# A new searched order for a planned one-core kernel, with VectorE and GpSimd kept apart in the search's model

## The chip, the cores and the metric

One core of a Trainium2 chip. The time is that of the core from the first to the last instruction plus launch, in device microseconds (us), median over a few runs. TensorE is called PE in the profile, VectorE DVE, ScalarE ACT, GpSimd POOL. A run is called slow when it is over 1.5% above the fastest run of the same kernel.

## The reference, cut

```python
# r, k, v, w: (4, 8, 768, 48); u: (8, 48)
for t in range(S):                         # linear attention with decay
    cur = einsum('bhd,bhe->bhde', u * k[t], v[t])
    y[t] = einsum('bhd,bhde->bhe', r[t], state + cur)
    state = w[t][..., None] * state + einsum('bhd,bhe->bhde', k[t], v[t])
x = y as (batch, seq, 384)
theta = x @ w_theta                        # wave mixing
y2 = w_tok_r @ (x * cos(theta)) + w_tok_i @ (x * sin(theta))
u = x + y2
out = u + relu(u @ w_ch)
```

The kernel splits each of the four batches into six chunks of 128 steps, numbered 0 to 23. Per chunk it takes a logarithm of the decay (ACT), cumulative sums of it (PE), exponentials of these (ACT), products with r and k (POOL), transposes and small matmuls (PE, copied and masked by DVE), a bonus term u*k*r, and the chunk's output x. Then theta, sine and cosine, the products z (DVE), token mixing, channel mixing, store.

## The kernel before

The program is not written in its final order. Every step is registered with durations and a priority; a planner simulates the engines while the kernel is built and so fixes the order on each engine, and for some steps which engine runs it.

```python
class Planner:
    def op(self, eng, dur, fn, deps=(), alloc=(), free=(), mode=None, prio=0.0, name="", alts=(), pen=0.0):
        key = self.key(name)                       # kind of step and batch: 'z@0', 'beta@0', ...
        penalty = self.penalty.get(key, ...)       # PENALTY: when to take the other engine
        ...
        prio += self.shift.get(key, ...)           # SHIFT: earlier or later in the order
    def order(self, window):
        ...
            first = min(cand, key=lambda q: q[0])          # the step that can start first in the model
            lim = first[0] + window.get(eng, 0.0)          # WIN: how long an engine may wait for a better one
            t, o, eng, dur, i = min((q for q in cand if q[2] == eng and q[0] <= lim),
                                    key=lambda q: (q[1].prio, q[1].i))
```

Each engine works through its queue in this order, and waits where the next step can't start yet. The other part is one accumulator of two PSUM banks, "cum". Its second bank also holds the eight columns of the bonus sums ("beta"), and the "fillers" write to it: matmuls whose result nobody uses, put into TensorE's gaps to keep its clock up. They are put in after the order is fixed, so the planner does not simulate them.

```python
pads["cum"] = [pps.tile([L, 2, 512], f32, tag="cum", name="cum")]
pads["beta"] = [pads["cum"][0][:, 1, DM:DM + H]]             # DM = 384, H = 8
...
def f_cum():                                                  # PE, L435 to L439
    nc.tensor.matmul(cm[:, 0, :DM], ...); nc.tensor.matmul(cm[:, 1, :DM], ...)
def f_exp():                                                  # ACT, L444: reads both banks
    nc.scalar.activation(get(a), get(cum)[:, :, :DM], AF.Exp)
def f_beta(...):                                              # PE, L775: bonus sums into cum's second bank
    nc.tensor.matmul(get(bt), lhsT=get(rkT)[:, j, :], rhs=ublk[:, j, :], ...)
o_bc = P.op("DVE", 0.08, f_rub, [o_beta], [], [bt], ..., name=f"bc{n}",
            alts=[("ACT", 0.1, f_rub_a, 0.0)])                # bonus copy: L780 on DVE, L783 on ACT
o_bon = P.op("POOL", 0.79, f_bon, [o_bc, o_v[i]], ...)        # bonus product, L788
wps = pads["cum"][0][:, 1, DM:]
def fill():                                                   # filler, L1073
    nc.tensor.matmul(wps, lhsT=warm[:, 0, :], rhs=warm[:, 1, :], start=True, stop=True)
```

## Time and profile before

| | before |
|---|---|
| median of 3 runs | 170.01 us (168.47 to 171.23) |
| span of the profiled run, mean granted clock | 168.1 us, 0.984 |
| VectorE busy in all / before 40 us | 132.3 / 26.9 us |
| logarithm of chunk 7 / exponential of chunk 6 start | 24.8 / 23.0 us |
| first z product starts | 38.1 us |

### The profile page before, as it was taken

How to read it: one execution, taken by the hardware profiler on the slowest of the kernel's cores; microseconds unless marked ns; L12 is line 12 of the kernel's file. 1: busy time of each engine (PE TensorE's matmuls, PEld its weight loads, DVE VectorE, ACT ScalarE, POOL GpSimd, SP SyncE). 2: the span in 40 equal slices, each digit the busy share in tenths (PEclk: the TensorE clock that was granted, in tenths of full speed). 3: DMA queues.
4: the chain of work that ended last, by engine and by line, in shares of the span. 5: the costliest groups of instructions: out<-in, count | busy, mean ns of one | idle time of the engine just before them, and what ended most of it. 6: DMA issues, size and time to landing. Idle time of an engine off the chain costs nothing.

```text
span 168.1 us, 5063 instructions
## 1 busy us (share of the span) xinstructions
PE 153.9 (92%) x1986; PEld 103.7 (62%) x1986; DVE 132.3 (79%) x287; ACT 116.0 (69%) x264; POOL 112.4 (67%) x133
## 2 busy tenths in 40 slices
PE   7997798995898999999999999999899999999981
PEld 7575476763665676657566677666566666666640
DVE  4506958899999988797899998899988997436361
ACT  3556585699889997667998696489979963932000
POOL 7198488997986689866367989999979921000000
PEclk9959999999999999999999999999999999999997
DMA  4999999897989999999999999897911101020312
GB/s 102 277 261 248 252 258 177 161 285 174 272 227 215 268 244 281 258 284 216 207 188 206 251 179 221 168 223 142 236 41 47 49 4 66 30 97 0 140 47 94
DMA packets 93769, 29.81 MB, mean 177 GB/s; under 512 B 88369, under 2 KB 92210, under 8 KB 93746
## 3 DMA queue, kind: packets, MB, share of 16 engines
q1 hardware_dynamic: 93344, 29.50, 79.2%
q8 instruction: 15, 0.25, 0.6%
q14 instruction: 8, 0.07, 0.2%
q10 hardware_dynamic: 402, 0.00, 0.1%
HBM read 24.78 MB, written 4.72 MB: 175 GB/s over the span
## 4 chain that ended last, share of the span: by engine, by line
PE 71%; DVE 11%; ACT 8%; POOL 3%; DMA 2%; issue 2%; ACTq 0%; POOLq 0%
PE bank L978 25%; PE bank L1005 7%; PE bank L941 4%; DVE sb_z L955 4%; PE cum L1073 3%; PE bank L611 3%; PE bank L548 3%; PE bank L992 2%; DMA in_w<-in_w_dram 2%; PE bank L606 2%; PE bank L530 2%; PE bank L532 2%; PE bank L632 2%; PE bank L1054 2%; PE cum L435 2%
## 5 line engine op out<-in xcount | busy, mean ns | idle before, releaser
L978 PE MATMUL bank<-sb_z,wtokT 128*128 128x384 bf16 x288 | 53.8, 326 | 0.0
L978 PEld LDWEIGHTS <-wtokT 128*128 128x128 bf16 x288 | 26.0, 98 | 14.9
L524 POOL TENSOR_TENSOR sb_bon<-sb_v,sb_rub 128x384 bf16<-128x384 bf16 x18 | 14.9, 829 | 13.5 <-DVE sb_rub L520 5.5
L955 DVE TENSOR_TENSOR sb_z<-x_all,sb_sc 128x768 bf16<-128x768 bf16 x24 | 20.2, 858 | 1.6 <-ACT sb_sc L949 1.6
L463 POOL TENSOR_TENSOR sb_q<-in_r,sb_a 128x384 bf16<-128x384 f32 x18 | 18.6, 1035 | 2.8 <-ACT sb_alt L449 2.4
L457 POOL TENSOR_TENSOR sb_k<-in_k,sb_a 128x384 bf16<-128x384 f32 x18 | 18.6, 1032 | 1.4 <-DMA in_k<-in_k_dram 1.4
L508 POOL TENSOR_TENSOR sb_ru<-in_r,u_bc 128x384 f32<-128x384 f32 x18 | 19.2, 1069 | 0.2
L987 DVE TENSOR_TENSOR sb_un<-bank,x_all 128x384 bf16<-128x384 f32 x24 | 13.3, 554 | 7.6 <-PE bank L978 7.3
L444 ACT ACTIVATE sb_a<-cum 128x768 f32<-128x768 f32 x18 | 14.8, 824 | 4.2 <-PE cum L439 2.7
L515 POOL TENSOR_TENSOR sb_ruk<-sb_ru,in_k 128x384 bf16<-128x384 f32 x16 | 17.2, 1075 | 0.5
L327 ACT ACT_TABLE_LOAD x12 | 15.4, 1283 | 1.5 <-PEq L1089 1.3
L1005 PE MATMUL bank<-wch,sb_uT 128*128 128x384 bf16 x72 | 15.5, 327 | 0.6 <-DVE sb_uT L999 0.5
L1010 DVE SCALAR_TENSOR_TENSOR sb_o<-bank,sb_un 128x384 f32<-128x384 f32 x24 | 13.2, 553 | 3.6 <-PE bank L1005 3.3
L1073 PE MATMUL cum<-warm 128*128 128x128 bf16 x106 | 11.6, 262 | 4.4 <-ACT sb_rub L783 1.8
L949 ACT ACTIVATE sb_sc<-bank,hpi 128x384 bf16<-128x384 f32 x24 | 14.7, 612 | 0.0
L941 PE MATMUL bank<-wth,sb_xT 128*128 128x384 bf16 x72 | 14.0, 326 | 0.3 <-ACT sb_sc L949 0.3
L536 DVE COPY sb_qkt<-bank 128x1024 bf16<-128x1024 bf16 x18 | 12.3, 684 | 1.6 <-PE bank L532 1.5
L946 ACT ACTIVATE sb_sc<-bank 128x384 bf16<-128x384 f32 x24 | 12.4, 516 | 1.4 <-PE bank L941 1.3
L996 ACT ACTIVATE sb_uT<-bank 128x384 bf16<-128x384 bf16 x14 | 7.0, 503 | 9.0 <-PE bank L992 8.9
L636 ACT ACTIVATE sb_xT<-bank 128x384 bf16<-128x384 bf16 x15 | 7.3, 496 | 8.3 <-PE bank L632 8.3
L553 DVE TENSOR_TENSOR sb_p<-bank,mask_exc 128x512 bf16<-128x512 f32 x18 | 12.3, 683 | 0.6 <-PE bank L548 0.5
L594 ACT ACTIVATE sb_S<-bank,sb_alt 128x48 bf16<-128x48 f32 x52 | 11.6, 323 | 1.7 <-PE bank L584 1.7
(135 smaller groups left out, 341.4 us busy)
## 6 DMA issues: line engine op xcount, KB each, us to landing
out_dram<-sb_o SPq DMA_DIRECT2D x24, 192.0 KB, 2.6
in_w<-in_w_dram SPq DMA_DIRECT2D x18, 192.0 KB, 4.9
in_r<-in_r_dram SPq DMA_DIRECT2D x18, 192.0 KB, 4.8
in_k<-in_k_dram SPq DMA_DIRECT2D x18, 192.0 KB, 4.5
in_v<-in_v_dram SPq DMA_DIRECT2D x18, 192.0 KB, 4.5
sb_w<-in_moe_w_tok_r_dram SPq DMA_DIRECT2D x6, 384.0 KB, 4.9
sb_w<-in_moe_w_tok_i_dram SPq DMA_DIRECT2D x6, 384.0 KB, 5.2
in_w<-in_w_dram SPq DMA_DIRECT2D x3, 384.0 KB, 5.0
```

The costliest lines, as they stand in the source:

```text
L327: nc.scalar.preload_act_table_set(name)
L444: nc.scalar.activation(get(a), get(cum)[:, :, :DM], AF.Exp)
L457: nc.gpsimd.tensor_tensor(get(kk)[:, :, :D], s["x_k"](), av(1), op=ALU.mult)
L463: nc.gpsimd.tensor_tensor(get(q)[:, :, :D], s["x_r"](), av(0), op=ALU.mult)
L508: nc.gpsimd.tensor_tensor(get(ru), s["x_r"](), u_bc, op=ALU.mult)
L515: nc.gpsimd.tensor_tensor(get(ruk), get(ru), s["x_k"](), op=ALU.mult)
L524: nc.gpsimd.tensor_tensor(get(bon), get(vb), get(rub).to_broadcast([L, H, D]), op=ALU.mult)
L941: nc.tensor.matmul(get(th), lhsT=get(s["xT"])[:, j, :], rhs=wth[:, j, :], start=(j == 0), stop=(j == NJ - 1))
L955: nc.vector.tensor_tensor(get(zb[b])[:, c], xb, get(sc), op=ALU.mult)
L978: nc.tensor.matmul(get(ac), lhsT=wtokT[:, q_, s_, ti, :], rhs=get(zb[b])[:, s_, q_, :], start=(s_ == 0 and q_ == 0), stop=(s_ == NCH - 1 a ...
L1005: nc.tensor.matmul(get(ml), lhsT=get(uT)[:, j, :], rhs=wch[:, j, :], start=(j == 0), stop=(j == NJ - 1))
L1073: nc.tensor.matmul(wps, lhsT=warm[:, 0, :], rhs=warm[:, 1, :], start=True, stop=True)
```

## The change

The intent: an order from a new search, in whose model a two-operand VectorE product and a GpSimd instruction exclude each other. What the program gets of it is other priorities (135 of 197 keys of SHIFT, 28 of 41 of PENALTY), other windows and load slacks, and a filler that stays off the bonus columns.

```diff
-    SHIFT = {... 'beta@0': 6.96, 'k@0': -9.79, 'ln@0': 5.4, 'v@0': 1.16, 'xc@0': 0.36, 'z@0': -4.98 ...}
+    SHIFT = {... 'beta@0': 10.46, 'k@0': -15.3, 'ln@0': 6.56, 'v@0': 6.14, 'xc@0': 3.41, 'z@0': -8.2 ...}
-    PENALTY = {... 'bc@0': -0.71 ...}          # bonus copies of the opening: on ACT
+    PENALTY = {... 'bc@0': 0.63 ...}           # ... on DVE
-    SLACK = (3.98, 6.1)
+    SLACK = (4.97, 6.65)
-    WIN = {'PE': 0.1, 'ACT': 0.11, 'DVE': 0.16, 'POOL': 0.39, 'SP': 0.1}
+    WIN = {'PE': 0.0, 'ACT': 0.27, 'DVE': 0.17, 'POOL': 0.0, 'SP': 0.38}
-    wps = pads["cum"][0][:, 1, DM:]
+    wps = pads["cum"][0][:, 1, DM + 2 * H:]
-        nc.tensor.matmul(wps, lhsT=warm[:, 0, :], rhs=warm[:, 1, :], start=True, stop=True)
+        nc.tensor.matmul(wps, lhsT=warm[:, 0, :], rhs=warm[:, 1, :L - 2 * H], start=True, stop=True)
```

(SHIFT and PENALTY are cut; "@0" is the first batch.)

More of the change, by code (lines that the diff above doesn't have):

```diff
@@ L212 @@
     OFF = {'ln': -2.2, 'cum': -2.1, 'exp': -2.05, 'alt': -2.04, 'q': -1.5, 'k': -1.45, 'v': -1.2, 'ru': -1.3, 'ruk': -1.2, 'rub': -1.2, 'bon': -1.1, 'tqk': -0.9, 'qkt': -0.9, 'p': -0.8, 'm0': -0.7, 'pc': -0.7, 'sel': -1.6, 'y': -0.5, 'x': -0.5, 'xt': -0.4, 'xc': -0.4, 'rk': -1.3, 'rkt': -1.2, 'rkc': -1.2, 'beta': -1.15}
-    SHIFT = {'M': -0.23, 'M@0': 3.78, 'M@1': -8.79, 'M@3': 4.37, 'Mp@0': 5.06, 'S': -3.32, 'S@0': 0.3, 'S@1': 4.4, 'S@3': -1.39, 'Sp@0': -0.82, 'alt': -2.71, 'alt@0': -6.46, 'alt@1': -5.24, 'alt@3': -1.0, 'bc@0': 2.73, 'beta@0': 6.96, 'bon': -7.28, 'bon@0': -11.25, 'bon@1': -1.68, 'bon@3': -15.43, 'cos': -4.6, 'cos@0': -8.64, 'cos@1': -3.05, 'cos@3': -4.08, 'cum': 2.98, 'cum@0': -0.21, 'cum@1': -0.34, 'cum@3': 0.03, 'cumo@0': -2.52, 'cump@0': 0.81, 'cwch': 2.19, 'cwch@1': 0.17, 'cwt': -0.63, 'cwt@1': -5.35, 'cwth': 0.26, 'cwth@1': -10.14, 'exk@0': 3.3, 'exp': -7.56, 'exp@0': -8.69, 'exp@1': -7.51, 'exp@3': -3.91, 'exq@0': -3.62, 'fin': 10.83, 'fin@0': 10.28, 'fin@1': 11.48, 'fin@3': 1.68, 'k': -2.66, 'k@0': -9.79, 'k@1': -1.84, 'k@3': 3.21, 'ldk': -0.07, 'ldk@0': 0.25, 'ldk@1': 0.18, 'ldk@3': -0.13, 'ldkp@0': -0.23, 'ldr': -0.52, 'ldr@0': -1.79, 'ldr@1': -1.7, 'ldr@3': -1.11, 'ldrp@0': -0.32, 'ldv': 0.27, 'ldv@0': 0.93, 'ldv@1': 0.57, 'ldv@3': 1.39, 'ldvp@0': 0.18, 'ldw': -1.63, 'ldw@0': -1.67, 'ldw@1': -2.55, 'ldw@3': -1.18, 'ldwp@0': -6.51, 'ln': -1.02, 'ln@0': 5.4, 'ln@1': -2.53, 'ln@3': 2.0, 'm': 1.57, 'm@0': 15.82, 'm@1': 14.98, 'm@3': 17.21, 'ml': 3.16, 'ml@0': -6.88, 'ml@1': -11.74, 'ml@3': -9.39, 'p': 4.22, 'p@0': 8.66, 'p@1': 17.51, 'p@3': 5.23, 'pc': 1.07, 'pc@0': 1.12, 'pc@1': -0.89, 'pc@3': -3.49, 'pp@0': -0.08, 'q': -0.33, 'q@0': -1.43, 'q@1': -1.77, 'q@3': 2.32, 'qkt': 1.93, 'qkt@0': 3.15, 'qkt@1': -5.42, 'qkt@3': -1.23, 'qktp@0': -4.05, 'rk@0': 4.47, 'rkc@0': 2.84, 'rkt@0': -3.15, 'ru': -2.75, 'ru@1': 3.2, 'ru@3': 4.03, 'rub': 1.54, 'rub@1': 3.87, 'rub@3': 6.62, 'ruk': -0.11, 'ruk@1': 4.75, 'ruk@3': 0.58, 'sel': 1.06, 'sel@0': 2.59, 'sel@1': 1.72, 'sel@3': -2.89, 'sin': 1.45, 'sin@0': 7.58, 'sin@1': 1.41, 'sin@3': 6.75, 'st': 0.43, 'st@0': -2.07, 'st@1': 5.27, 'st@3': -5.11, 'th': -5.14, 'th@0': -13.68, 'th@1': -11.99, 'th@3': -7.44, 'toE': -2.74, 'toE@0': 1.79, 'toE@1': 3.28, 'toE@3': 5.51, 'toS': -2.78, 'toS@0': 4.03, 'toS@1': 1.52, 'toS@3': 0.01, 'tok': -3.84, 'tok@0': -14.49, 'tok@1': -16.93, 'tok@3': -11.95, 'tqk': -0.37, 'tqk@0': -7.47, 'tqk@1': -3.98, 'tqk@3': -6.14, 'ubc': 3.86, 'ubc@1': -1.26, 'ublk@1': 12.81, 'ubm': 3.03, 'ubm@1': -0.13, 'uc': -4.81, 'uc@0': -0.8, 'uc@1': 1.76, 'uc@3': 5.44, 'un': 2.42, 'un@0': 3.41, 'un@1': 1.64, 'un@3': 0.26, 'ut': -3.32, 'ut@0': -11.88, 'ut@1': -17.65, 'ut@3': -16.65, 'v': 1.33, 'v@0': 1.16, 'v@1': 4.38, 'v@3': 2.97, 'wch': -0.56, 'wch@1': 4.47, 'wev': 2.67, 'wev@1': 3.64, 'wt': 0.86, 'wt@1': 1.37, 'wth': 0.4, 'wth@1': 0.12, 'wtr': 0.92, 'wtr@1': 4.43, 'x': 1.16, 'x@0': -4.58, 'x@1': -2.03, 'x@3': 1.47, 'xc': 1.62, 'xc@0': 0.36, 'xc@1': 6.08, 'xc@3': 2.79, 'xp@0': -4.33, 'xt': 0.48, 'xt@0': -1.77, 'xt@1': 4.35, 'xt@3': 2.35, 'y': -0.38, 'y@0': -2.78, 'y@1': 3.73, 'y@3': 5.0, 'yp@0': -0.46, 'z': -1.82, 'z@0': -4.98, 'z@1': -4.18, 'z@3': -2.79}
@@ L214 @@
-    PENALTY = {'S': 1.09, 'S@0': 1.12, 'S@1': -0.94, 'S@3': -3.96, 'bc@0': -0.71, 'bon@0': 2.38, 'cwch': -1.71, 'cwch@1': 2.81, 'cwt': 1.34, 'cwt@1': 3.16, 'cwth': 1.85, 'cwth@1': 0.93, 'k': 9.17, 'k@0': 10.47, 'k@1': 3.58, 'k@3': 6.59, 'pc': -1.22, 'pc@0': -2.79, 'pc@1': -4.91, 'pc@3': -5.2, 'qkt': 3.99, 'qkt@0': -0.11, 'qkt@1': 0.97, 'qkt@3': 1.62, 'qktp@0': 2.76, 'rk@0': 7.24, 'rkc@0': 3.74, 'ruk': -1.87, 'ruk@1': -0.54, 'ruk@3': -9.82, 'uc': 1.64, 'uc@0': -1.68, 'uc@1': 4.04, 'uc@3': -0.06, 'wev': -0.04, 'wev@1': -7.81, 'xc': -0.05, 'xc@0': -0.64, 'xc@1': 0.26, 'xc@3': 1.02, 'xp@0': 0.98}
+    SHIFT = {'M': -0.23, 'M@0': 3.78, 'M@1': -7.76, 'M@3': 1.6, 'Mp@0': 6.07, 'S': -3.32, 'S@0': 0.3, 'S@1': 3.47, 'S@3': -5.43, 'Sp@0': 0.87, 'alt': -2.71, 'alt@0': -7.8, 'alt@1': -4.87, 'alt@3': -2.49, 'bc@0': 0.71, 'beta@0': 10.46, 'bon': -7.28, 'bon@0': -10.68, 'bon@1': -0.95, 'bon@3': -19.71, 'cos': -4.6, 'cos@0': -3.77, 'cos@1': 0.94, 'cos@3': -1.14, 'cum': 2.98, 'cum@0': -0.21, 'cum@1': -5.7, 'cum@3': -2.37, 'cumo@0': -3.74, 'cump@0': 5.67, 'cwch': 2.19, 'cwch@1': -3.57, 'cwt': -0.63, 'cwt@1': -7.7, 'cwth': 0.26, 'cwth@1': -9.37, 'exk@0': 2.24, 'exp': -7.56, 'exp@0': -5.72, 'exp@1': -9.58, 'exp@3': -4.88, 'exq@0': -3.97, 'fin': 10.83, 'fin@0': 9.22, 'fin@1': 9.71, 'fin@3': -0.86, 'k': -2.66, 'k@0': -15.3, 'k@1': -4.27, 'k@3': 1.55, 'ldk': -0.07, 'ldk@0': 0.25, 'ldk@1': 0.13, 'ldk@3': 0.89, 'ldkp@0': -0.42, 'ldr': -0.52, 'ldr@0': -1.79, 'ldr@1': -0.62, 'ldr@3': 0.15, 'ldrp@0': -2.11, 'ldv': 0.27, 'ldv@0': 0.93, 'ldv@1': 0.81, 'ldv@3': 0.8, 'ldvp@0': -0.39, 'ldw': -1.63, 'ldw@0': -1.67, 'ldw@1': -1.52, 'ldw@3': -1.0, 'ldwp@0': -8.52, 'ln': -1.02, 'ln@0': 6.56, 'ln@1': -3.97, 'ln@3': 0.5, 'm': 1.57, 'm@0': 17.11, 'm@1': 14.33, 'm@3': 18.59, 'ml': 3.16, 'ml@0': -5.3, 'ml@1': -10.15, 'ml@3': -6.56, 'p': 4.22, 'p@0': 8.66, 'p@1': 21.13, 'p@3': 7.31, 'pc': 1.07, 'pc@0': 1.12, 'pc@1': -2.9, 'pc@3': -4.38, 'pp@0': -3.94, 'q': -0.33, 'q@0': -2.14, 'q@1': -1.73, 'q@3': 0.86, 'qkt': 1.93, 'qkt@0': 8.58, 'qkt@1': -1.62, 'qkt@3': 1.84, 'qktp@0': -3.17, 'rk@0': 3.53, 'rkc@0': 2.59, 'rkt@0': -3.32, 'ru': -2.75, 'ru@1': -1.29, 'ru@3': 5.05, 'rub': 1.54, 'rub@1': 7.06, 'rub@3': 6.83, 'ruk': -0.11, 'ruk@1': 5.43, 'ruk@3': 5.09, 'sel': 1.06, 'sel@0': 2.59, 'sel@1': 3.09, 'sel@3': -0.42, 'sin': 1.45, 'sin@0': 8.73, 'sin@1': 1.09, 'sin@3': 6.7, 'st': 0.43, 'st@0': 1.55, 'st@1': 5.34, 'st@3': -2.17, 'th': -5.14, 'th@0': -22.54, 'th@1': -14.23, 'th@3': -11.46, 'toE': -2.74, 'toE@0': 0.01, 'toE@1': 1.24, 'toE@3': 5.55, 'toS': -2.78, 'toS@0': 0.29, 'toS@1': -2.5, 'toS@3': -1.98, 'tok': -3.84, 'tok@0': -11.27, 'tok@1': -17.01, 'tok@3': -7.89, 'tqk': -0.37, 'tqk@0': -7.23, 'tqk@1': -2.21, 'tqk@3': -2.4, 'ubc': 3.86, 'ubc@1': -1.35, 'ublk@1': 6.96, 'ubm': 3.03, 'ubm@1': 5.81, 'uc': -4.81, 'uc@0': -1.6, 'uc@1': 0.56, 'uc@3': 1.71, 'un': 2.42, 'un@0': -1.03, 'un@1': -3.78, 'un@3': -2.8, 'ut': -3.32, 'ut@0': -10.4, 'ut@1': -12.13, 'ut@3': -11.86, 'v': 1.33, 'v@0': 6.14, 'v@1': 9.23, 'v@3': 8.57, 'wch': -0.56, 'wch@1': 4.81, 'wev': 2.67, 'wev@1': 8.97, 'wt': 0.86, 'wt@1': 1.89, 'wth': 0.4, 'wth@1': 1.94, 'wtr': 0.92, 'wtr@1': 1.41, 'x': 1.16, 'x@0': -4.58, 'x@1': -4.12, 'x@3': 5.65, 'xc': 1.62, 'xc@0': 3.41, 'xc@1': 8.02, 'xc@3': 4.74, 'xp@0': 0.3, 'xt': 0.48, 'xt@0': -5.9, 'xt@1': -0.32, 'xt@3': -1.61, 'y': -0.38, 'y@0': -2.78, 'y@1': 2.48, 'y@3': 1.82, 'yp@0': -0.56, 'z': -1.82, 'z@0': -8.2, 'z@1': -5.11, 'z@3': -6.98}
@@ new lines @@
+    PENALTY = {'S': 1.09, 'S@0': 1.12, 'S@1': -5.12, 'S@3': -6.5, 'bc@0': 0.63, 'bon@0': 2.28, 'cwch': -1.71, 'cwch@1': 8.23, 'cwt': 1.34, 'cwt@1': 1.5, 'cwth': 1.85, 'cwth@1': 0.89, 'k': 9.17, 'k@0': 10.96, 'k@1': 1.14, 'k@3': 7.87, 'pc': -1.22, 'pc@0': -2.79, 'pc@1': -7.95, 'pc@3': -6.99, 'qkt': 3.99, 'qkt@0': 4.29, 'qkt@1': 4.07, 'qkt@3': 4.08, 'qktp@0': 3.13, 'rk@0': 5.41, 'rkc@0': 3.16, 'ruk': -1.87, 'ruk@1': -1.1, 'ruk@3': -8.83, 'uc': 1.64, 'uc@0': -3.91, 'uc@1': 4.0, 'uc@3': -1.83, 'wev': -0.04, 'wev@1': -5.78, 'xc': -0.05, 'xc@0': -0.32, 'xc@1': -0.06, 'xc@3': 0.94, 'xp@0': 3.9}
```

## The prediction

> **What bounds the kernel now.** I read the page's first two parts, then the busy time of each engine by 10 us stretch, then the chain of waits, and last the single instructions around a slow product. The page first:
>
> ```profile
> PE 153.9 (92%) x1986; PEld 103.7 (62%) x1986; DVE 132.3 (79%) x287; ACT 116.0 (69%) x264; POOL 112.4 (67%) x133
> ...
> PE   7997798995898999999999999999899999999981
> DVE  4506958899999988797899998899988997436361
> POOL 7198488997986689866367989999979921000000
> ```
>
> TensorE (PE) is the busiest engine by far, and from slice 15 (60 us) on it has no hole. By stretch (columns: PE, PE weight loads, DVE, ACT, POOL busy us with counts, then granted clock, DMA share, GB/s):
>
> ```profile
> 30.00:40.00 10.00, 9.13 (x179) 6.68 (x178) 9.15 (x17) 9.14 (x18) 10.00 (x11) 1.00 0.90 206
> 40.00:50.00 10.00, 7.74 (x131) 5.56 (x130) 10.00 (x20) 8.71 (x19) 9.04 (x10) 1.00 0.99 238
> 50.00:60.00 10.00, 9.03 (x136) 6.42 (x136) 9.21 (x21) 9.67 (x22) 6.48 (x8) 1.00 1.15 258
> 140.00:150.00 10.00, 10.00 (x82) 6.07 (x80) 5.59 (x12) 5.58 (x11) 0.00 (x0) 1.00 0.23 81
> ```
>
> At 40 to 50 us PE is idle 2.26 us while DVE has no idle at all: there the vector engine sets the pace. "Busy" also hides slack, because matmul ends are modelled. So I counted, from the trace's matmuls, the time that their columns need: N/2.4 GHz + 2.5 ns each, at least 25 ns (formula below). Useful work is 137.9 us, the warm-up matmuls of the filler line L1073 another 5.9. Useful us per stretch: 1.7 in 0-10; 7.05, 7.67, 9.14, 6.01, 8.06 in the five stretches of 10-60; 95.1 in the 100 us of 60-160; 3.1 in the last 8.1. The span of 168.1 thus has 30.2 us in which PE did not advance: 8.3 at the start, 12.1 in 10-60, 4.9 in 60-160, 5.0 at the end. Start (first loads, masks) and end (last channel matmul, result, store) are outside what an order can change much. About 17 us are what a reordering can fight for, two thirds of it before 60 us.
>
> The chain of waits says what stands there (start, length, what):
>
> ```profile
> 38.15 2.37 DVE sb_z L955 x2
> ...
> 43.17 2.15 DVE sb_z L955 x2
> ...
> 83.68 1.20 DVE sb_z L955
> 84.87 0.47 DVE sb_un L987
> 85.34 0.80 DVE sb_z L955
> ```
>
> These are the products x * (cos, sin), both inputs in SBUF. The same instruction by tile (min/median/max ns), and one slow case in the timeline:
>
> ```profile
> L955 DVE TENSOR_TENSOR sb_z<-x_all,sb_sc x24: 543/840/1396, 38.1 to 148.6; 128x768 bf16<-128x768 bf16 x24
> ```
>
> ```profile
> 53.31 1.00 POOL L457 TENSOR_TENSOR sb_k<-in_k,sb_a 128x384 bf16<-128x384 f32 x1
> 53.34 1.40 DVE L955 TENSOR_TENSOR sb_z<-x_all,sb_sc 128x768 bf16<-128x768 bf16 x1 [0.38 <-ACT sb_sc L949]
> ...
> 54.28 1.31 POOL L515 TENSOR_TENSOR sb_ruk<-sb_ru,in_k 128x384 bf16<-128x384 f32 x1
> ```
>
> POOL started 0.03 us earlier; the product took 1.40 instead of 0.54, ending 0.42 after POOL's; the next POOL product, begun just before POOL's first ended, took 1.31 instead of 1.00. Alone (after 140 us, POOL empty) the products take 0.55 to 0.56.
>
> **What the Trainium skill says.** "SBUF — State Buffer", section "Who interferes with whom": a VectorE instruction with two SBUF inputs contends with a GpSimd instruction that reads SBUF, and the later one blocks until the first is done. The trace agrees (0.54 to 1.40, and 1.00 to 1.31 for the POOL side, which loses about 0.3, not a whole product). So the model behind the change is right in kind. "TensorE: Matmul & The Clock Gate", section "Wait — 56ns, not 53.3ns?": start to start N/2.4 GHz plus about 2.5 ns when warm, not under about 25 ns; for 384 columns that is 162.5 ns, and the chain's six-matmul pieces of L978 take 0.97 or 0.98, 162 each: agrees. Same page, "Part 1: The HAM clock gate": PE needs about 3.4 us of activity to run at full clock; here the granted clock is 0.95 and 0.88 in the first two stretches and 1.00 from 20 us to 160, so filler has little left to win.
>
> **The change part by part.** No matmul of the result is added or taken away. Only order and the choice of engine change. I compared both built programs engine by engine and gave each instruction the mean of its row in the profile before.
>
> 1. Engines. DVE gains six small bonus copies of 128x8 (0.12 each is my estimate, from the 0.18 that they took on ACT), one wide copy (0.68), three xT copies, two uT copies (0.35 each), and loses one ruk product (0.84), two S products and one pair-xT copy (0.35 each): 0.7 + 0.7 + 1.75 - 0.84 - 1.05 = +1.3 us. ACT: -6 x 0.18 - 1.02 - 3 x 0.50 - 2 x 0.50 + 0.5, and eight more of the four-piece S scalings at about 0.22 net: -2.3 us. POOL +1.0 (one ruk). None of this binds by sum; DVE's is the wrong way in 30-60 us.
>
> 2. Positions. Summing means (0.545 for an unblocked z) up to a landmark: DVE work ahead of the first z grows from 27.9 to 31.3 us, ahead of the third from 32.1 to 33.0, ahead of the sixth (the last of the first batch) from 42.2 to 44.0. On ACT the sixth sine stands at 44.8 before and 44.5 after. POOL's last bonus product goes from 115.8 to 116.9. On PE the useful columns ahead of the first token-mixing group fall from 32.4 to 31.3 us; from the last theta group to the end they go from 16.6 to 15.1. The last ten token groups stand at exactly the same place. So the plan is locally shuffled, not restructured.
>
> 3. The lock. Of the 24 products the mean is 858, alone 545: 7.5 us of DVE lost. POOL has about 14 products near 1.31 or 1.2 instead of 1.00: some 4 us. But only what is on the chain counts: the six z quoted there take 6.5 us for a free 3.3, an excess of 3.25. POOL is without a hole in 30-40, so a z must meet some POOL product there whatever the order; a plan that knows the lock can only choose who waits and put DVE work with one SBUF input beside POOL. I take half: -1.6 us.
>
> 4. Against it, DVE's +1.8 us ahead of the sixth z, in a stretch where DVE is full. But six of the copies moved to it replace waits on ACT, and work put ahead of z is work that no longer follows it. I charge a third: +0.6.
>
> 5. Filler. It writes 112 columns rather than 128 and leaves the bonus area of the accumulator bank alone; 111 instead of 106 of them: 111 x 49 ns = 5.5 instead of 5.9 us, all in gaps. One might expect the following wait to go:
>
> ```profile
> PE cum L1073 <- ACT sb_rub L783: 1.8, 5, 0.7
> ```
>
> The built program says no: after the change six fillers still wait for the bonus copy, only now on DVE (semaphore targets L780). So 1.8 us of PE waits stay, about as long, behind another queue. Credit 0; these waits lie between 20 and 42 us.
>
> 6. The middle: 4.9 us lost in 60-160, of which 2.0 in 110-130 where the chain runs through five POOL products (5.7 us, 0.9 of it blocking). I credit -0.4.
>
> Sum: -1.6 + 0.6 - 0.4 = -1.4 us, on 170.0: 168.6 us.
>
> **The rivals.** (a) The gain is swallowed: once z is earlier, PE is already full from 60 us, and the saved DVE time turns into waits of DVE for PE (un already waits 7.3 us for L978). For it: 95% column use in 60-160. Against: PE had 4.0 us of holes in 40-50. Time 169.5 to 170. (b) The whole search pays: better interleaving takes a third of the 12.1 us before 60 us, PE saturates by 50 us. For it: ACT does one more chunk's exponential before the first table switch, so POOL has work during the sines. Against: DVE has no idle to give there, and more work. Time 165 to 166.5. (c) The small copies on a full DVE queue hold the fillers, and useful matmuls stand in order behind these; or a plan fitted to a model misses the real load landing times (input loads took 4.5 to 4.9 us from issue, DMA share about 1.0 until 120 us). Time 171 to 173.
>
> **Range and chances.** The sum of 1.4 us is 0.8%, and the three runs of before differ by 1.6% among themselves, so "within 2%" is by far likeliest. Faster by over 2% needs 3.4 us, a fifth of all that is open: rival (b), 0.14. Slower by over 2%: 0.05. Eight in ten: 166.2 to 170.8.
>
> **What would show it.** Step 3: the mean of L955 falls from 858 to near 700, and the z pieces in the chain shrink. Step 4: DVE still full in 40-50. Step 5: a row of L1073 waiting for DVE sb_rub of 1 to 3 us. Step 6: fewer POOL products at 1.31. Step 2: useful PE work in 40-50 above 6.0 and in 60-160 near 95. It is wrong if L955 gets no shorter, or if PE's gain before 60 us reappears as idle after it, or if the loss in 10-60 falls below 9 us.

## More of the kernel before

"Busy" of VectorE is the time in which some instruction of it ran, each moment counted once. The main lines of the profile are in the prediction. These two rows of the costliest groups and two of the view by stretches are needed besides (rows: busy us and mean ns of one, then idle time of the engine ahead of them and what ended it; stretches: width, then busy us of PE, PE weight loads, DVE, ACT, POOL, granted clock, DMA share, GB/s):

```profile
L788 POOL TENSOR_TENSOR sb_bon<-sb_v,sb_rub 128x384 bf16<-128x384 bf16 x6 | 5.2, 882 | 3.4 <-ACT sb_rub L783 3.4
L1073 PE MATMUL cum<-warm 128*128 128x128 bf16 x106 | 11.6, 262 | 4.4 <-ACT sb_rub L783 1.8 <-DVE warm L296 1.1 <-ACT sb_a L706 0.9
```

```profile
0.00:40.00 40.00, 34.27 (x575) 25.53 (x576) 26.86 (x78) 26.49 (x59) 31.55 (x50) 0.96 1.01 219
40.00:168.10 128.10, 119.67 (x1414) 78.13 (x1411) 105.42 (x210) 89.48 (x206) 80.87 (x84) 0.99 0.73 164
```

So VectorE sits idle for 13.1 us of the first 40, and for 128.1 - 105.4 = 22.7 us of the rest.

## The result, and the profile after

| | before | after |
|---|---|---|
| median | 170.56 us (168.47 to 171.23, 4 runs) | 179.2 us (177.06 to 182.25, 4 runs) |
| ratio | | 1.0497, interval 1.036 to 1.0633 |

A ratio is the mean time of one kernel's fast runs over that of the other's of the same rounds, so not quite the ratio of these medians. The changed kernel is 5% slower. It also scatters more: two of its four runs are slow, with granted clocks of 0.92 and 0.93, against 0.97 in the fast two. The profiled run was a slow one (span 180.4, clock 0.92), so I read the profile of the run e1_again below, the same kernel in a fast run: span 176.0 us, clock 0.981. It is 7.9 us longer than before.

First the same stretches as above, of the changed kernel:

```profile
0.00:40.00 40.00, 32.38 (x486) 22.46 (x486) 21.02 (x71) 21.26 (x47) 29.36 (x49) 0.92 1.04 227
40.00:176.00 136.00, 124.89 (x1511) 82.58 (x1505) 113.60 (x224) 93.72 (x214) 82.87 (x86) 1.00 0.68 153
```

VectorE was busy for 21.0 us instead of 26.9 before 40 us, and for 134.6 instead of 132.3 in all. After 40 us it is idle for 136.0 - 113.6 = 22.4 us, as before (22.7). That closes the account of the span: 5.8 us more idle time in the opening, 2.3 us more work, 0.3 less idle time later, 7.9 with rounding. ScalarE lost about as much in the opening (21.3 against 26.5). From 40 us on both kernels keep VectorE at 19.2 of 20 us up to 60, so what it misses in the opening it never makes up. TensorE shows the same from its side: counted as in the prediction, its useful work had reached 39.6 us at time 60 in the kernel before and 34.6 in the changed one, and the next 60 us add 56.6 and 55.7. Up to 160 us it is 95.1 and 92.4: of the 7.9 us, about 5 are lost before 60 us and most of the rest after 120.

Now the opening by single instructions. In the timeline (start, us, engine, line, what; in brackets the idle time ahead and what ended it), ScalarE of the kernel before took the logarithm of chunk 7 at 24.84 us, and GpSimd the bonus products of the chunks 2 and 3 in one go:

```profile
24.84 0.52 ACT L430 ACTIVATE sb_lw<-in_w 128x384 bf16<-128x384 f32 x1
...
27.50 1.61 POOL L788 TENSOR_TENSOR sb_bon<-sb_v,sb_rub 128x384 bf16<-128x384 bf16 x2 [0.56 <-ACT sb_rub L783]
```

ScalarE of the changed kernel reached that logarithm (31.36) after this:

```profile
27.66 0.81 ACT L444 ACTIVATE sb_a<-cum 128x768 f32<-128x768 f32 x1 [3.32 <-POOL sb_k L733]
28.36 0.17 ACT L449 ACTIVATE sb_alt<-cum 128x4 f32<-128x4 f32 x1
28.41 0.50 ACT L917 ACTIVATE sb_xT<-bank 128x384 bf16<-128x384 bf16 x1
29.09 0.49 ACT L766 ACTIVATE sb_rkT<-bank 128x384 bf16<-128x384 bf16 x1 [0.18 <-PE bank L762]
29.48 0.93 ACT L741 ACTIVATE sb_v<-in_v 128x384 bf16<-128x384 f32 x2
30.30 1.15 ACT L393 ACTIVATE wth<-sb_w 128x1152 bf16<-128x1152 f32 x1
31.36 0.51 ACT L430 ACTIVATE sb_lw<-in_w 128x384 bf16<-128x384 f32 x1
```

The view names a GpSimd product as what ended the 3.32 us, but the exponential's own input, the cumulative sums, ended on TensorE only at 27.6: their logarithm came 2.7 us later than before (23.81 against 21.07), and they stand behind the first output products, where the old order has them in front. (That the GpSimd product is not the cause e14 below shows: there this exponential ran at 25.91, before the product began at 26.83.) Then an xT copy, which the old order leaves to VectorE, two v casts, which the old order has later, and a weight cast, which is ahead in both, stand before the logarithm. The cumulative sums of chunk 7, and in TensorE's queue behind them the bonus sums of chunk 3, come 6.4 and 5.0 us later than before (32.1 against 25.7, 32.7 against 27.7).

Next, the shared bank. In VectorE's waits (total us, times, longest) the changed kernel has rows that the old one has not, or, the first, with 0.3 us only:

```profile
DVE x_all L905 <- PE bank L895: 4.1, 2, 3.2
DVE sb_rub L780 <- ACT sb_a L444: 2.3, 2, 2.1
DVE sb_rub L780 <- ACT sb_a L709: 0.8, 1, 0.8
...
DVE sb_rub L780 <- ACT sb_a L706: 0.6, 1, 0.6
```

A bonus copy on VectorE waits for ScalarE's exponential, though it needs nothing of it. Both read the bank of the accumulator, and the built program lets the engines take turns there in program order. That such turns are needed is what the Trainium skill, "PSUM — Partial Sum Buffer", section "PSUM bank collisions raise a hardware error", says: two engines that touch one bank in the same quadrant of 32 partitions at once raise an error, also when both read and at different columns (copy and exponential here span all 128 partitions). What the turns cost, traces show. The plan did not know of them. Its own start times, which the program computes while it is built, have the copy run inside the exponential:

| step | plan before | plan after | real after |
|---|---|---|---|
| exponential of chunk 8 | 29.72 to 30.42 | 29.03 to 29.73 | 35.87 to 36.68 |
| bonus copy of chunk 4 | 34.47 to 34.57 (ACT) | 29.19 to 29.27 (DVE) | 36.78, after 2.14 us idle |

The plan as a whole foresaw no starvation either: computed in the same way, it ends at 158.0 us before and 159.1 after, and leaves VectorE idle for 14.9 and 15.1 us before 40. So by the planner's own durations and dependences the new order loses about 1 us of the 7.9. The rest comes from what the plan leaves out, as the turns and the fillers, or has wrong; beyond those two the runs don't tell what.

The chain of waits of the changed kernel (start, length, what) shows what hangs on that copy:

```profile
35.87 0.82 ACT sb_a L444
36.69 0.03 issue
36.71 0.02 DVEq L780
36.73 0.04 issue
36.78 0.18 DVE sb_rub L780
36.95 0.04 issue
37.00 0.44 PE cum L1073 x3
37.44 0.32 PE bank L887 x4
37.76 0.64 PE bank L890 x2
38.40 0.32 PE bank L887 x4
38.72 0.64 PE bank L890 x2
39.36 0.80 PE bank L895 x31
40.16 1.01 DVE x_all L905 x2
```

Exponential, copy, three fillers that wait for the copy, and behind the fillers, in order on TensorE, the output products of the chunks 2 and 3, for which VectorE waits until 40.16. Those products started at 29.6 in the kernel before. TensorE's clock had fallen as well: four matmuls of L887 took 0.32 us here and 0.17 in the chain of before. The rows of the changed kernel that answer to those two of before:

```profile
L955 DVE TENSOR_TENSOR sb_z<-x_all,sb_sc 128x768 bf16<-128x768 bf16 x24 | 20.8, 895 | 1.4 <-ACT sb_sc L949 1.4
...
L1073 PE MATMUL cum<-warm 128*128 128x112 bf16 x111 | 11.2, 262 | 7.1 <-DVE sb_rub L780 4.5 <-DVE warm L296 1.1 <-ACT sb_a L706 0.9
...
L788 POOL TENSOR_TENSOR sb_bon<-sb_v,sb_rub 128x384 bf16<-128x384 bf16 x6 | 5.0, 828 | 6.3 <-DVE sb_rub L780 6.3
```

The fillers' wait for the bonus copy went from 1.8 to 4.5 us, GpSimd's from 3.4 to 6.3. And what the search was after did not come over the whole kernel: the mean z product takes 895 ns (873 in the slow profile) instead of 858, though the six of the first batch got shorter (step 3 below). The first z was planned for 37.8 us and ran at 47.5; before, for 34.9, and ran at 38.1. A plan that is 10 us late meets other GpSimd instructions than the ones it was arranged around; that this is why the products got no shorter is my reading and not shown by itself.

### The profile page after: what moved, and what is told of

Read it like the earlier page. It is cut to its first block, busy times and chain, and to the rows that moved or that the text cites. A ratio compares the mean times of both kernels' runs of the same rounds, so it can differ in the third digit from the quotient of the medians.

```text
span 180.4 us, 5092 instructions
## 1 busy us (share of the span) xinstructions
PE 161.7 (90%) x1991; PEld 108.6 (60%) x1991; DVE 134.6 (75%) x295; ACT 115.2 (64%) x261; POOL 112.4 (62%) x134
## 4 chain that ended last, share of the span: by engine, by line
PE 69%; DVE 19%; ACT 6%; issue 3%; DMA 2%; ACTq 0%; DVEq 0%
PE bank L978 23%; DVE sb_z L955 7%; PE bank L1005 7%; PE bank L941 3%; PE bank L548 3%; PE bank L611 3%; PE bank L992 3%; PE cum L1073 2%; DMA in_w<-in_w_dram 2%; DVE sb_qkt L536 2%; PE cum L435 2%; PE cum L691 2%; PE bank L632 2%; PE bank L584 2%; PE bank L815 2%
## 5 line engine op out<-in xcount | busy, mean ns | idle before, releaser
L978 PE MATMUL bank<-sb_z,wtokT 128*128 128x384 bf16 x288 | 54.5, 330 | 0.6 <-DVE sb_z L955 0.5
L978 PEld LDWEIGHTS <-wtokT 128*128 128x128 bf16 x288 | 26.5, 98 | 17.0 <-issue 1.8
L524 POOL TENSOR_TENSOR sb_bon<-sb_v,sb_rub 128x384 bf16<-128x384 bf16 x18 | 15.0, 841 | 19.0 <-ACT sb_v L470 12.3
L444 ACT ACTIVATE sb_a<-cum 128x768 f32<-128x768 f32 x18 | 14.7, 816 | 11.7 <-PE cum L439 6.6
L955 DVE TENSOR_TENSOR sb_z<-x_all,sb_sc 128x768 bf16<-128x768 bf16 x24 | 20.3, 873 | 2.3 <-ACT sb_sc L949 2.3
L508 POOL TENSOR_TENSOR sb_ru<-in_r,u_bc 128x384 f32<-128x384 f32 x18 | 18.7, 1039 | 0.0
L1073 PE MATMUL cum<-warm 128*128 128x112 bf16 x111 | 11.6, 266 | 7.9 <-DVE sb_rub L780 4.5
L515 POOL TENSOR_TENSOR sb_ruk<-sb_ru,in_k 128x384 bf16<-128x384 f32 x17 | 17.9, 1056 | 0.2
L594 ACT ACTIVATE sb_S<-bank,sb_alt 128x48 bf16<-128x48 f32 x60 | 13.2, 313 | 2.2 <-PE bank L584 2.2
L1073 PEld LDWEIGHTS <-warm 128*128 128x128 bf16 x111 | 9.5, 127 | 8.3 <-issue 6.9
L946 ACT ACTIVATE sb_sc<-bank 128x384 bf16<-128x384 f32 x24 | 12.3, 511 | 3.0 <-PE bank L941 3.0
L553 DVE TENSOR_TENSOR sb_p<-bank,mask_exc 128x512 bf16<-128x512 f32 x18 | 12.3, 683 | 1.8 <-PE bank L548 1.8
L536 DVE COPY sb_qkt<-bank 128x1024 bf16<-128x1024 bf16 x18 | 12.3, 681 | 0.9 <-PE bank L532 0.9
L804 DVE COPY sb_qkt<-bank 128x1024 bf16<-128x1024 bf16 x6 | 6.0, 994 | 8.6 <-PE bank L815 6.1
```

The source lines that it names most:

```text
L508: nc.gpsimd.tensor_tensor(get(ru), s["x_r"](), u_bc, op=ALU.mult)
L515: nc.gpsimd.tensor_tensor(get(ruk), get(ru), s["x_k"](), op=ALU.mult)
L524: nc.gpsimd.tensor_tensor(get(bon), get(vb), get(rub).to_broadcast([L, H, D]), op=ALU.mult)
L536: nc.vector.tensor_copy(get(qkt), get(tp))
L955: nc.vector.tensor_tensor(get(zb[b])[:, c], xb, get(sc), op=ALU.mult)
L978: nc.tensor.matmul(get(ac), lhsT=wtokT[:, q_, s_, ti, :], rhs=get(zb[b])[:, s_, q_, :], start=(s_ == 0 and q_ == 0), stop=(s_ == NCH - 1 a ...
```

## The experiments

The theory after the result: the order of the opening starves VectorE, in part through turns in the shared bank. The rivals: the bonus copies' engine alone; the fillers; a lower granted clock; or a loss spread over the whole order.

### The change taken apart: the same kernel again, and three of its parts

```diff
  e1_again: the changed kernel as it is
  e2_after_fill128: changed order, old filler
-    wps = pads["cum"][0][:, 1, DM + 2 * H:]     ... rhs=warm[:, 1, :L - 2 * H]
+    wps = pads["cum"][0][:, 1, DM:]             ... rhs=warm[:, 1, :]
  e3_before_fill112: the kernel before with the new filler (the reverse edit)
  e4_after_rub_act: changed order, the six bonus copies of the opening on ACT, at the same places
+            if re.match(r"bc\d", o.name):
+                o.pick, o.eng = 1, "ACT"
```

> The changed kernel once more, for a profile in the fast state beside the kernel before on one chip. All theories: 1.03 to 1.065 of the kernel before. Clock theory (W: the early work is too thin to keep TensorE at full clock): the granted clock is under 0.9 in at least one of the stretches 20-30 and 50-60 us in the fast profile too, where the kernel before has 1.00. Order theory (O): useful columns by 60 us stay some 5 us behind those of before even where the clock is 1.00.

> The changed order with the old filler of 128 columns, nothing else moved. W in its narrow form (the narrower filler is what lets the clock drop): the ratio to the kernel before falls from about 1.05 to under 1.02, clock 1.00 in 20-30 us. O: stays 1.035 to 1.06.

> The old order with the new filler of 112 columns on columns clear of the bonus. W in its narrow form: slower, 1.03 to 1.06 of the kernel before, clock well below 1 in 20-30 us. O: 0.99 to 1.01, clock as before.

> The changed order, with the six small bonus copies done by ScalarE at the same places of the program rather than by VectorE. Theory R (these copies wait behind VectorE's products, and fillers, bonus products on GpSimd and the next matmuls wait for them): at least half of the loss goes, ratio 1.00 to 1.025, the 4.5 us of fillers waiting for them falls under 2. If the loss is spread over the whole order (O) or comes from the filler's width (W): 1.035 to 1.06.

Measured: e1_again 179.02 us, ratio 1.0555 (1.0458 to 1.0652); e2 177.73 us, 1.0435 (1.034 to 1.0531); e3 170.69 us, 1.0061 (1.0009 to 1.0114); e4 178.04 us, 1.0364 (1.0289 to 1.044). e1_again fits both the clock and the order theory: the granted clock of 20 to 30 us is 0.83 (1.00 before), and useful work is 5 us behind at 60 us. It decides nothing between them; e8 below does. The narrower filler is no part of the gain or of the loss that would matter: in either order it costs, if anything, a little (the intervals of e1 and e2 overlap). The loss is the order's. Moving the copies back to ScalarE takes back about two of its 5.5 points (two fast runs only), not the half or more that theory R asked for. Points here and below are differences to the 1.0555 of e1_again; the first measurement, 1.0497, would make each 0.6 smaller.

### The shared bank and the fillers

```diff
  e5_after_own_bank, e6_before_own_bank: bonus sums of the opening in a PSUM bank that is free at that time
+            for b in o.alloc:
+                if b.pool == "beta":
+                    j = max(n for n, q in enumerate(ops) if b in q.free)
+                    x = spare(i, j)                    # a bank that no step holds between i and j
+                    if x is not None:
+                        b.pool, b.slot, b.shape, b.dtype = "bank", x, [128, 8], FP32
  e9_after_all_banks: besides, each filler writes to a free bank
+        dst = pps.tile([L, L], f32, tag=f"bank{x}", name=f"bank{x}")[:, :wps.shape[-1]]
  e7_after_few_fill, e8_before_few_fill: only the 33 fillers that lead
-    FUNTIL = 130.0
+    FUNTIL = 0.0
  e10_after_both: e5's and e7's edits together
```

> The changed order with the six bonus sums put into an accumulator bank of their own that is free at that place of the program, so that they share none with the cumulative sums; order and engines as in the changed kernel. Theory T (turn-taking: in the changed order the bonus sums stand between a cumulative sum and its exponential, in the same bank, so exponential, bonus copy, filler and next cumulative sum wait for each other): ratio to the kernel before falls from 1.055 to 1.01-1.03, VectorE's bonus copy waits for no exponential, granted clock over 0.9 in 20-40 us, first table switch back from 42.7 to under 39 us. Order theory without the bank (O): 1.04-1.06.

> The same move of the bonus sums (five of six; no free bank for the last) in the old order. T: there the bonus sums and their copies stand before the next cumulative sum and on the engine of the exponential, so little waits: 0.985-1.005. If the shared bank costs the same in any order: 0.96-0.98.

> As the own-bank run of the changed order, and the fillers too go to a free bank, so that none waits for an exponential or a bonus copy. T: a little better than that run, 1.00-1.025, idle of TensorE before fillers from 7.9 to under 2 us. O: 1.04-1.06.

> The changed order with the 33 fillers at the start alone, none later. If the clock is what costs (W): 1.07 or more, clock 0.5 over most of 10-40 us. If the fillers' waits cost more than the clock that they hold: 1.03-1.05.

> The kernel before without fillers after the 33 that lead. If fillers are a burden in any order (they stand in the shared bank's turns): ratio 0.98 to 0.995. If the changed order alone suffers from them (its 3.4 per cent against 5.5): 0.995 to 1.01, and a lower clock in the opening.

> The changed kernel with both remedies: the bonus sums in banks of their own and no fillers after the 33 that lead. If the two add: idle of VectorE before 40 us of 14 to 15.5 and a ratio of 1.015 to 1.027. If both relieve the same wait (fillers behind a bonus copy): 1.028 to 1.036, as each alone.

Measured: e5 176.15 us, 1.0336 (1.0271 to 1.04). e6 (a free bank was found for five of the six) 169.29 us, 0.9965 (0.9947 to 0.9984). e7 175.38 us, 1.0339 (1.028 to 1.0397). e8 170.6 us, 1.005 (0.9987 to 1.0112). e10 173.39 us, 1.0273 (1.0201 to 1.0344). e9 is a failed edit: it took 187.09 us, 1.1009, because every filler asked for a tile of its own, and fillers in a row came mostly 0.27 to 0.31 us apart instead of about 0.05; that they waited for each other's tiles is likely, not shown. It tells nothing of the shared bank.

The bonus sums' place in the shared bank carries about two of the changed kernel's 5.5 points and 0.4% of the old kernel's time. (e5 fell between the two bands forecast. The waits of its copies for exponentials are gone, but its fillers still wait 4.2 us, now for the exponentials.) The fillers that stand in these turns carry as much in the changed order; without them the granted clock of the first 40 us falls from 0.92 to 0.79, and the kernel is faster all the same. e8 says it more directly: its clock up to 40 us is 0.91, as low as the changed kernel's, and the old order takes 1.005. So the clock is not what makes the loss. In the old order, taking the fillers away wins nothing. The two remedies seem to take away largely the same wait: alone 2.2 points each, together 2.8, not 4.4. (e10's 1.0273 lies between the bands forecast, and its interval overlaps those of e5 and e7.) Of the waits that the kernel before has not, or hardly, VectorE keeps these before 41 us in e10 (its lines are numbered 25 higher):

```profile
DVE x_all L930 <- PE bank L920: 3.6, 2, 2.4
DVE sb_rub L805 <- PE bank L800: 1.7, 2, 1.0
```

The waits of the copies for exponentials are gone, those for the output products (4.1 in the changed kernel) are not: half of the loss is there without these turns and fillers.

### Which part of the order

First I mixed the planner's keys. h3 is the changed kernel with the old keys of the first batch, old WIN and SLACK; h4 is the reverse, with the old filler.

```diff
  h3: SHIFT, PENALTY: every key that ends in '@0' from the kernel before; WIN, SLACK from it too
  h4: the same from the changed kernel into the kernel before
```

> The changed kernel, but the planner's keys of the first batch, its windows and its slacks are taken from the kernel before: the first 30 us are then planned nearly as before (bonus copies on ScalarE, the sixth cumulative sum ahead of the first output products), the rest by the changed keys. If the loss sits in the order of the opening: ratio 0.99 to 1.02, and useful TensorE work of 38 to 41 us by 60 us. If it sits in the later keys or in the order as a whole (any order not tuned on the chip loses): 1.03 or more.

> The reverse: the kernel before with the changed keys of the first batch, the changed windows and slacks, old filler. If the opening's order carries the loss: ratio 1.03 to 1.06, useful TensorE work of 33 to 37 us by 60 us. If the later keys do: 0.99 to 1.02.

Measured: h3 183.02 us, 1.0685 (1.0597 to 1.0774), half its runs slow; h4 176.37 us, 1.0421 (1.0348 to 1.0494). h4 came out as the theory said, h3 against it. But neither is what I had taken it for: in h3 the cumulative sums of chunk 7 ran at 35.9 us, further from the old order (25.7) than those of the changed kernel. The keys act on all steps that compete, so a part of the keys does not give back a part of the order. So I made the planner replay: the first steps of the other kernel's plan, in exactly its order and on its engines, then free.

```diff
  g1_after_opening_before (215 steps, planned 0 to 38 us); g2_before_opening_after (218 steps)
+    OPENING = ("ublk:0 ldwp0:0 ... wev00:1 ldv7:0").split()       # step:engine choice
...
+                if o.name in first_ops:
+                    end, t, eng, dur, i = pl[first_ops[o.name] if len(pl) > 1 else 0]
                 cand.append((t, o, eng, dur, i))
+            if turn < len(queue):
+                cand = [q for q in cand if q[1].name == queue[turn]]
+                turn += 1
```

> The changed kernel, its planner made to take the first 215 steps (planned 0 to 38 us) exactly in the order and on the engines of the kernel before, then free with the changed keys. Account: span = VectorE's busy total + its idle time before 40 us + about 22.7 us of its idle time after. If the opening's order carries the loss: idle before 40 us falls from 19 to 12.5 to 14.5 us, VectorE's total is 133 to 134.5 (its plan has 0.6 more than the changed one's), so a span of 168.5 to 171.5 and a ratio of 1.00 to 1.02. If it lies later or in any untuned joint: 1.03 to 1.06.

> The reverse: the first 218 steps (planned 0 to 38 us) exactly as the changed plan has them, then free with the keys of the kernel before; old filler. This plan puts 4.3 us more on VectorE than the kernel before, so its total should be about 136.5 to 138. If the opening's order carries the loss: idle before 40 us of 17.5 to 19.5, span 176 to 180, ratio 1.05 to 1.07. If the opening is harmless: idle before 40 us of 13 to 14.5, ratio 1.02 to 1.04 from the load alone.

Measured: g1 173.16 us, 1.0221 (1.0149 to 1.0292); g2 178.37 us, 1.0523 (1.0442 to 1.0604). The first stretch of each, g1 first:

```profile
0.00:40.00 40.00, 34.55 (x569) 24.70 (x570) 25.35 (x77) 24.91 (x57) 29.83 (x49) 1.00 1.03 219
```

```profile
0.00:40.00 40.00, 32.13 (x493) 23.58 (x494) 21.55 (x72) 21.37 (x47) 28.50 (x48) 0.87 1.00 218
```

VectorE's 25.4 and 21.6 us go with the opening and not with the kernel: 26.9 and 21.0 are those of its two parents. The old opening takes 3.3 of the 5.5 points off the changed kernel; the new one puts 5.2 on the old kernel, that is some 9 us, of which 3.1 us are VectorE work that this plan has more (135.4 against 132.3). g1's ratio is a little above the band that I had given; it keeps 1.7 us more VectorE work than the kernel before and 1.5 more of idle time in the opening.

### The copies alone, and one step alone

```diff
  e13_before_rub_dve: the kernel before, bonus copies on VectorE at the same places
+            if re.match(r"bc\d", o.name):
+                o.pick, o.eng = 0, "DVE"
  e11_after_cum_first: the changed kernel, cumulative sums of chunk 6 ahead of the first output products
+        ops.insert(at("yp0"), ops.pop(at("cum6")))
  e14_after_yp_behind: the same swap the other way round
+        ops.remove(q)                          # q = yp0, p = cum6
+        ops.insert(ops.index(p) + 1, q)
```

> The kernel before, its six small bonus copies of the opening on VectorE instead of ScalarE, at the same program places. If the copies' place on VectorE's queue makes the loss by itself: VectorE idle before 40 us of 15.5 to 18 instead of 13.1, ratio 1.02 to 1.035. If only their six times 0.17 us count: ratio 1.00 to 1.01.

> The changed kernel, with one TensorE step moved: the cumulative sums of the seventh chunk stand ahead of the first output products instead of behind them; the number of fillers is the same. If the exponential of that chunk, 4.7 us later than in the kernel before, carries the loss of the opening: it starts by about 25.5 us instead of 27.7, the first rotation product 2 us earlier, ratio 1.035 to 1.045. If other waits stand behind it at once: 1.05 to 1.06, as the changed kernel.

> The changed kernel with the first output products (yp0) put behind the cumulative sums of the seventh chunk on TensorE, both behind the logarithm that these need. The sums should start by about 24.8 us instead of 27.0 and their exponential by 25.5 instead of 27.7. If this one step carries much of the opening's loss: VectorE idle before 40 us of 16.5 to 17.8 instead of 19.0, ratio 1.04 to 1.048. If the order of the other steps holds the opening all the same: idle of 18.3 to 19.3 and 1.05 to 1.058.

(The expectations count chunk 6 as the seventh.) Measured: e13 169.7 us, 1.0028 (0.9963 to 1.0092). e11 gave a wrong result, relative error 0.026: the logarithm that the sums read stood later in the program, so they read the tile before it was written. Its time, 180.99 us, counts for nothing. e14 moves the output products instead: correct, 178.69 us, 1.0575 (1.0511 to 1.0638).

e13: in the old order the copies' engine costs nothing that can be told from zero. Its VectorE waits have no row of a copy that waits for an exponential: where bonus sums stand ahead of an exponential that reads the bank, the old order has the copies of the chunks 2 to 5 ahead of it too, while the changed order has four of its six copies behind it. Yet e13's fillers wait 3.6 us for the copies and its GpSimd 5.0, against 4.5 and 6.3 in the changed kernel. So these waits alone need not cost anything; that the work behind them decides is my reading. e14 is the lesson of the opening in one picture. ScalarE's timeline (lines numbered 6 higher):

```profile
25.91 0.81 ACT L450 ACTIVATE sb_a<-cum 128x768 f32<-128x768 f32 x1 [1.40 <-POOL sb_q L735]
26.62 0.17 ACT L455 ACTIVATE sb_alt<-cum 128x4 f32<-128x4 f32 x1
29.53 0.49 ACT L923 ACTIVATE sb_xT<-bank 128x384 bf16<-128x384 bf16 x1 [2.74 <-PE bank L919]
```

The exponential came 1.8 us earlier, as meant (25.91 against 27.66). But the next long step in ScalarE's queue is the xT copy, which needs those output products; the 3.32 us of idle time became 1.40 and 2.74, the next logarithm came 1.7 us later (33.07), and the kernel was no faster. One step out of place is not the cause; the queues fit each other or they don't.

### The account over all runs, and the fastest kernel

```diff
  e15_own_bank_again: e6 once more, five rounds
```

> The kernel before with the bonus sums in banks of their own, once more with five rounds. If the gain of the first look is real: ratio 0.994 to 0.998. If it was the chip's scatter: 0.998 to 1.003.

Measured: 168.17 us against 169.23, 0.9954 (0.9907 to 1.0). With e6's 0.9965 it is the one version that beats both kernels, by some 0.4%; the interval of the second set touches 1.

VectorE in the profiled runs (span, busy total, idle before and after 40 us, granted clock up to 40 us):

| kernel | span | busy | idle before 40 | idle after 40 | clock to 40 | ratio |
|---|---|---|---|---|---|---|
| e15 | 166.1 | 132.4 | 10.9 | 22.8 | 1.00 | 0.995 |
| e6 | 167.2 | 132.7 | 12.0 | 22.6 | 0.96 | 0.997 |
| e8 | 167.8 | 132.6 | 12.3 | 22.9 | 0.91 | 1.005 |
| before | 168.1 | 132.3 | 13.1 | 22.7 | 0.96 | 1 |
| e13 | 169.0 | 131.9 | 13.8 | 23.3 | 0.96 | 1.003 |
| e3 | 169.1 | 132.3 | 14.1 | 22.8 | 1.00 | 1.006 |
| g1 | 171.4 | 134.0 | 14.7 | 22.8 | 1.00 | 1.022 |
| e10 | 173.0 | 133.9 | 16.9 | 22.2 | 0.91 | 1.027 |
| e7 | 173.1 | 134.3 | 16.1 | 22.7 | 0.79 | 1.034 |
| e5 | 174.3 | 134.4 | 17.6 | 22.4 | 0.83 | 1.034 |
| h4 | 175.0 | 135.3 | 16.6 | 23.1 | 0.87 | 1.042 |
| e1_again | 176.0 | 134.6 | 19.0 | 22.4 | 0.92 | 1.056 |
| e14 | 176.1 | 134.6 | 18.8 | 22.7 | 0.91 | 1.058 |
| g2 | 176.9 | 135.4 | 18.4 | 23.1 | 0.87 | 1.052 |

That the three terms add up to the span is arithmetic. What the runs show is that the last hardly moves (22.2 to 23.3 here), so these kernels differ by VectorE's work and by what it misses before 40 us. The table has every correct run with a fast profile but the failed edit e9, which has 31.6 us after 40. The slow profiles at clocks of 0.91 and 0.92, h3, e4 and the first one of the changed kernel, don't obey: they have 26.4, 26.2 and 26.9 us after 40; e2's, at 0.98, has 23.3. e15 and e6 are one kernel and show 10.9 and 12.0 before 40, so a difference of 1 us there means nothing.

## Why the prediction was wrong, point by point

**The step that failed is step 2**, "So the plan is locally shuffled, not restructured", with the way it was found: the orders were compared by the work that stands ahead of a landmark. The difference that it found was right to the decimal: 27.9 to 31.3 us of VectorE work ahead of the first z, 3.4 more; up to the first z VectorE was in fact busy for 24.9 and 28.3 us, counted without overlap. But the first z came 9.4 us later, and the other 6.1 us are idle time (13.1 before, 19.2 after), for which the sum of the prediction has no term. Whether queues wait for each other can't be seen in sums of work. It asked for a walk along the queues of the opening: cumulative sums behind output products, the logarithm behind an xT copy, with the bank's turns and the fillers in it. The plan is such a walk without these two and with modelled durations, and it has 0.2 us more idle time before 40 us, not 5.8. g1 and g2 show that this opening makes most of the loss.

**Step 5** had the mechanism and not the size: fillers wait for the bonus copy on VectorE, row of 1 to 3 us foreseen, 4.5 measured. "Credit 0" left out what follows: output products stand behind these fillers, and the copies themselves wait 3.7 us for exponentials. e5 and e7 each give back 2.2 points.

**Step 4** charged a third of 1.8 us. VectorE's total rose by 2.3 us (six copies, 1.0 us of instruction time, are within it), and as its idle time after 40 us stayed the same (22.7 and 22.4), all of it appears in the span's account.

**Step 3** took half of the excess of the lock (VectorE's products blocked by GpSimd's) as won, -1.6 us. In the first batch that came true: its six z products took 5.2 us in all instead of 6.8 (summed over the instructions of L955 in the two traces). The twelve of the next two batches lost more, 12.8 instead of 10.2, so the mean over all went from 858 to 895 ns: "L955 gets no shorter", a sign of being wrong, came true. Nor was it the lock that decided: in g2 the mean is 785 ns, and g2 is 5.2% slower. **Step 6**, -0.4 in the middle: useful TensorE work between 60 and 160 us fell from 95.1 to 92.4, though GpSimd products of 1.15 us and more did become fewer (10 instead of 14).

**Step 1**, no engine bound by its sum, holds as arithmetic, and misled in the same way as step 2. (The chain's six-matmul pieces of L978 take 1.08 us as well as the 0.97 or 0.98 that the prediction quotes; no step rests on it.)

**The rivals.** (c) named both things that happened, small copies that hold fillers with useful matmuls behind them, and a plan fitted to a model that misses the real times, but gave them 171 to 173 us, and a chance of 0.05 to anything over 2% slower. (a) and (b) did not happen. The test that I had set, "the loss in 10-60 falls below 9 us", was for a larger gain; the loss there went from 12.1 to 17.1 us.

**What stays open.** 2.2% remain with the old opening (g1): about half more VectorE work, the rest within the scatter of the opening's idle time or in the joint at 38 us. Within the opening, turns and fillers are shown to carry about half (e10); which waits make the other half is read from the traces and not tested one by one. And why the lock was met more often in the later batches is argued from the drift of the plan, not shown.

## What to carry to other kernels

When only an order changes, don't add up the work ahead of a landmark: follow, queue by queue, which step waits for which in the stretch before the engines fill up; what VectorE and TensorE missed there was not made up later here. A searched order is as good as its model of waits; look for pairs that the plan lets overlap and the program does not, here two readers of one accumulator bank. And moving one step to where the better order has it can just trade one wait for another, so test an order by replaying a whole stretch of it.

## What the Trainium skill lacked or had wrong

- "PSUM — Partial Sum Buffer": it says that engines must not touch a bank at once, not what the turns cost. Here the bonus copies waited 3.7 us for exponentials in the same bank and fillers 4.5 us for the copies; banks of their own took the changed kernel from 1.0555 to 1.0336 of the time before, and the old kernel to 0.9954 and 0.9965.
- "TensorE: Matmul & The Clock Gate": it tells how to keep the clock up, not that warm-up matmuls can cost more than they win when they share a queue and a bank with useful work. In the changed order, without those after the lead, the clock up to 40 us fell from 0.92 to 0.79 and the ratio from 1.0555 to 1.0339; in the old order taking them away gave 1.005, an interval that includes 1.
- No page tells how to judge, before it runs, what a changed order does to waits across queues: 3.4 us more work ahead of the first z came with 6.1 us more idle time.
